# Turned products of the last two channel groups laid out by partition in DRAM, and read back by four transfers each

## The chip, the cores and the metric

The kernel runs on one core of one Trainium2 chip. The metric is device time in microseconds (us), the median of several executions; before the change it is 266.08 us (three runs, 264.74 to 267.07). The core has a matrix engine (PE, with its weight loads shown apart as PEld), a vector engine (DVE), a scalar engine (ACT), GpSimd (POOL) and a sync engine (SP), which here issues nearly all transfers; sixteen DMA engines carry them.

## The reference

Two branches work on the same input of 2048 positions by 512 channels, and a gate per position mixes them. Branch a convolves each channel with a kernel built from 128 complex exponentials; branch b is linear attention with 32 heads.

```python
x = A_u
g = _sigmoid((x * gate_w).sum(-1, keepdims=True))
P = jnp.exp(logdA[:, :, None] * l[None, None, :])
K = jnp.einsum("dn,dnl,dn->dl", Cc, P, dB).real
...
y = irfft2(rfft2(u, padded) * rfft2(K, padded))[..., :L] + u * Dskip
...
b = _B_ref(x, B_wqkv, B_w_phi, B_wo)
return g * a + (1 - g) * b
```

## The kernel before

The convolution is done by a Fourier transform in two stages of matrix products. The 512 channels are worked in quarters Q of 128; units of 32 channels (0 to 15) make the convolution kernels (`kgen`), and `transform` carries a group of channels through the rest. The first three quarters go as groups of nd = 128 channels. The last quarter is cut into three groups by `g.LAST`: units 12 and 13 (nd = 64), unit 14 (nd = 32), both "far", and unit 15 (nd = 32), "near".

In `transform` a group goes through these steps, named as the profile names their tiles:

- `psB` on PE (L192), copied to `XK`, multiplied on DVE with the spectrum of the input, `XUX`, to give `t` (L1231, for nd = 32 in two halves, L1234). `XUX` is loaded from DRAM by `load`, two transfers of 256 KB for each of four parts of a quarter (L1183, for the last quarter L1185, where each of 128 partitions takes one run of 2 KB).
- `psz` on PE (L1263) is the first stage of the inverse transform, evicted by ACT to `Zr`. For a far group the product has to be turned: what lies in one partition as many rows r has to lie with r over the partitions. This goes through DRAM: `fw` writes `Zr` to the tensor `Zd` (L1277 or L1279), `fr` reads `Zd` back into `ZT` (L1290 or L1292). A group of nd channels has 1024/nd rows r in one write, so nd = 64 makes two writes and nd = 32 one. The near group takes another way (L1304) and has no round trip.
- `psy` on PE (L1342, L1348) is the second stage, from `ZT`; DVE multiplies by the gate into `xT` (L1373), and `st` writes the result to `out` (L1387). The attention part of the output is written by L992.

In 128 partitions p stands for the pair (x, t), x of 4 and t of 32. Before the change the two layouts of `Zd` are: for nd = 128 and 64 ("byrow") [r, x, t, d], written in runs of nd numbers and read by four transfers of 32 partitions, each partition one long run; for nd = 32 [t, x, r, d], written with x as the outermost of two partition dimensions and read by two transfers of 64 partitions.

The order of all work is written out by hand: `Plan` holds a list of nodes and the string `ORDER`, and every engine issues its instructions in that order. SP therefore takes transfers strictly one after another; a transfer whose wait isn't met holds those behind it. Eight completion semaphores are handed round among the transfers, so a transfer can also wait for the one eight places ahead of it. `XUX` has three buffers, `Zr` two and `ZT` one (shared with another tile, "ax").

Of the kernel before, what the change touches and what calls it, by code (L numbers as in the profile page):

```python
# [13 lines left out]
BF16 = mybir.dt.bfloat16  # L14
# [1042 lines left out]
def plan_conv(P, nc, g, psum, r):  # L1057
# [8 lines left out]
    def evict2(name, get, deps, ps):  # L1066
        out = []
        for k in range(2):
            out.append(P.add(("ACT", "DVE"), name, lambda k=k: P.copy(*get(k)), [ps] + deps[k] + out, drop=(["psum"] if k else [])))
        return out  # L1070
# [119 lines left out]
    def transform(XA, ready, Q, off, nd, far, Ls, last, co=0, free=True, split=False):  # L1190

        F = Bag()
        ng, ns, nj, nt = nd // 2, 1024 // nd, min(16, 1024 // nd) if far else 8, min(32, 2048 // nd)
# [4 lines left out]
        ov = g.out2d[:, 128 * (Q - pair) + lo:128 * Q + off + nd].rearrange("(q j c) d -> c q j d", q=32, j=16, c=4)  # L1198
        bS = xT[:, :, Q, :]
        if far:  # L1200
            byrow = nd > 32
            F.Zd = g.dram.tile([32, 4, 32, nd], BF16, name=f"Zd{Q}_{off}")
        tn, zn, rn, wn = [], [], [], []
        for r0 in range(0, 32, ns):
            box = Bag()
# [44 lines left out]
            x = evict2("XK", xk, [[], []], b) if split else [evict("XK", xk, [b])]  # L1250
# [24 lines left out]
            def fw(r0=r0, box=box):  # L1275
                if byrow:
                    nc.sync.dma_start(out=F.Zd[r0:r0 + ns].rearrange("r x t d -> (x t) r d"), in_=box.Z[:])  # L1277
                else:
                    nc.sync.dma_start(out=F.Zd[:, :, r0:r0 + ns, :].rearrange("t x r d -> x t (r d)"), in_=box.Z[:].rearrange("p r d -> p (r d)"))  # L1279
                box.Z = None  # L1280
            z = P.add("PE", "psz", fi, [tn[-1]] + ([z] if r0 else []), take=[psq, "Zr"], drop=(["r8"] if (r0 + ns) % nt == 0 else []), rw=("TI", ""))
            zn.append(evict("Zr", fe, [z] + zn[-1:]))
            wn.append(P.dma("zw", 0.45, 2.0, fw, [zn[-1]], drop=["Zr"], move=0.9))

        def fr(th):
            if th == 0:
                F.Z = g.fpool.tile([128, 4096], BF16, name="ZT", tag="ax", bufs=g.P.k["ax"])[:, 0:32 * nd].rearrange("p (t d) -> p t d", d=nd)
            if byrow:
                for x in (2 * th, 2 * th + 1):
                    nc.sync.dma_start(out=F.Z[32 * x:32 * x + 32], in_=F.Zd[:, x])  # L1290
            else:
                nc.sync.dma_start(out=F.Z[64 * th:64 * th + 64], in_=F.Zd[:, 2 * th:2 * th + 2].rearrange("t x r d -> (x r) t d"))  # L1292
        for th in range(2 if far else 0):
            rn.append(P.dma("zr", 0.6, 2.0, lambda th=th: fr(th), wn + [n.issue for n in rn[-1:]], take=(["ax"] if th == 0 else []), move=max(1.2, 2.8 * nd / 128 + 0.1), cnt=2 if byrow else 1))
        box = Bag()

        def iz(k2, box=box):
# [23 lines left out]
        for j0 in range(0, 16, nj):  # L1321
            box = Bag()
# [66 lines left out]
            if Q < 3:  # L1389
                ya = [P.add("PE", "pya", pya, [sq] + [n for b in range(j0 // 4, min(3, j0 // 4 + 2)) for n in g.ot[b]] + ([y] if j0 else []), take=[psq], rw=("diagD", ""))]  # L1390
            y = P.add("PE", ("psy%d" if far else "psyn%d") % nd, py, ya + (rn[:1 + (j0 + nj - 1) // 8] if far else zn) + [sq] + (late if Q == 3 else []) + ([y] if j0 else []),
                      take=[] if ya else [psq],
# [11 lines left out]
    for h in range(6):  # L1404
        for u in (2 * h, 2 * h + 1):
            if u in g.PHASES and u:
                phase(range(u, g.PHASES[u]))
        if h % 2 == 0:
            XA = Bag()
            XA.nd, XA.off, XA.drop, done = 128, 0, True, []  # L1410
        done = done + kgen((2 * h, 2 * h + 1), XA, h % 2 == 0)
        if h % 2:
            transform(XA, done, h // 2, 0, 128, True, [load(h // 2, p) for p in range(4)], False)
# [7 lines left out]
    for k, (units, far) in enumerate(g.LAST):  # L1421
        XA = Bag()
        XA.nd, XA.off, XA.first = 32 * len(units), 32 * (units[0] - 12), first
        XA.drop = units[-1] == 15
        done = kgen(units, XA, True, units in g.SPLIT)
        first = XA.first
        end = units[-1] == 15
        off = 32 * (units[0] - 12)
        transform(XA, done, 3, off, XA.nd, far, L[off // 64 * 2:off // 64 * 2 + 2], end, off % 64, units[-1] % 2 == 1, units in g.SPLIT)
# [204 lines left out]
```

## Time and profile before

| | before |
|---|---|
| median of the runs | 266.08 us (264.74 to 267.07) |
| profiled execution: device time | 267.7 us |
| profiled execution: span, first to last instruction | 265.9 us |
| mean granted PE clock | 0.923 |
| busy share of the span: DVE, ACT, PE | 87%, 83%, 74% |
| DMA: moved, mean rate | 36.19 MB, 136 GB/s |
| DMA packets, of them under 512 bytes | 67087, 46308 |

The span is what the views of the profile divide up; 1.8 us of the device time lie outside it. All times in a view count from the span's start. DVE and ACT are busy nine tenths of the time up to about 240 us; the last 25 us have low shares on every engine, and there the chain of waits goes over transfers and PE.

### The profile page before, as it was taken

The numbers are of one execution on the slowest core, as the hardware profiler recorded it, in microseconds if no ns is written. First come the engines' busy times: TensorE is split into PE (matmuls) and PEld (weight loads), VectorE is DVE, ScalarE is ACT, GpSimd is POOL, SyncE is SP. The second block draws the span as 40 slices with busy tenths as digits, with TensorE's granted clock in tenths as the row PEclk, the third lists the DMA queues.
The fourth block names the chain that finished last, engine by engine and source line by source line (L and its number), as shares of the span: only waits on it lengthen the run. The fifth ranks groups of instructions, "written<-read, shape, count | busy, mean of one in ns | idle before, by whom it ended". The sixth has DMA issues, their size and how long they took to land.

```text
span 265.9 us, 10075 instructions
## 1 busy us (share of the span) xinstructions
PE 195.7 (74%) x4492; PEld 134.0 (50%) x4512; DVE 231.8 (87%) x314; ACT 221.2 (83%) x305; POOL 11.7 (4%) x22
## 2 busy tenths in 40 slices
PE   0386899999947568887487666799886787993840
PEld 0275566755735333445355354575764566762630
DVE  6899799898799998999999999999999999934440
ACT  7877998888899999999999999999999988553000
POOL 4750000000000000000000000000000000000000
PEclk9997999999985798999959999999999999999575
DMA  6799000361721677406150575639775989586675
GB/s 193 132 202 208 1 4 2 115 160 39 226 61 58 177 223 206 137 6 164 48 148 7 156 194 147 154 88 231 189 210 129 217 207 223 94 218 146 140 92 90
DMA packets 67087, 36.19 MB, mean 136 GB/s; under 512 B 46308, under 2 KB 62820, under 8 KB 66660
## 3 DMA queue, kind: packets, MB, share of 16 engines
q1 hardware_dynamic: 65988, 35.42, 55.0%
q8 instruction: 35, 0.57, 1.0%
q10 hardware_dynamic: 1056, 0.13, 0.3%
q14 instruction: 8, 0.07, 0.1%
HBM read 22.17 MB, written 13.37 MB: 134 GB/s over the span
## 4 chain that ended last, share of the span: by engine, by line
DVE 30%; ACT 27%; PE 27%; issue 6%; DMA 6%; SPq 1%; DVEq 0%; ACTq 0%
ACT cs L68 6%; DMA XUX<-XUd 6%; PE pk L705 5%; PE vp L753 4%; DVE A L1098 3%; DVE t L1231 3%; ACT E L68 3%; ACT XA L145 3%; ACT Eq L68 3%; PE psB L612 2%; PE kvp L770 2%; ACT L65 2%; PE psA L587 2%; ACT XK L145 2%; DVE XAu L147 2%
## 5 line engine op out<-in xcount | busy, mean ns | idle before, releaser
L1098 DVE TENSOR_TENSOR A<-Ctab,Dtab 128x2048 bf16<-128x2048 bf16 x32 | 38.6, 1218 | 0.4 <-PE kps L179 0.4
L68 ACT ACTIVATE cs<-args 128x1024 bf16<-128x1024 f32 x32 | 31.0, 1072 | 0.0
L179 PE MATMUL kps<-R,A 128*32 128x64 bf16 x1536 | 17.3, 201 | 5.9 <-DVE A L1098 1.8
L179 PEld LDWEIGHTS <-A 128*32 128x32 bf16 x1536 | 15.6, 116 | 10.1 <-issue 4.1
L1116 DVE TENSOR_TENSOR R<-E,cs 128x2048 bf16<-128x2048 bf16 x16 | 19.5, 1218 | 0.6 <-ACT E L68 0.5
L1120 DVE TENSOR_TENSOR R<-E,cs 128x2048 bf16<-128x2048 bf16 x16 | 19.5, 1216 | 0.0
L145 ACT CAST Zr<-psz 128x1024 bf16<-128x1024 f32 x15 | 15.6, 1040 | 4.3 <-issue 3.4
L1263 PE MATMUL psz<-t,TI 128*128 128x512 bf16 x53 | 14.8, 379 | 5.7 <-DVE t L1234 2.6
L68 ACT ACTIVATE Ek<-pk 128x512 bf16<-128x512 f32 x32 | 16.7, 603 | 2.6 <-PE pk L705 2.5
L145 ACT CAST XA<-psA 128x1024 bf16<-128x1024 f32 x15 | 15.1, 1043 | 3.1 <-PE psA L186 3.1
L1231 DVE TENSOR_TENSOR t<-XUX,XK 128x2048 bf16<-128x2048 bf16 x14 | 16.9, 1216 | 0.4 <-ACT XK L145 0.4
L753 PE MATMUL vp<-WW,xT 128*128 128x512 bf16 x58 | 16.3, 406 | 1.0 <-issue 0.8
L68 ACT ACTIVATE E<-args 128x1024 bf16<-128x1024 f32 x16 | 16.8, 1059 | 0.2 <-PE args L1042 0.2
L68 ACT ACTIVATE Eq<-pq 128x512 bf16<-128x512 f32 (+1 forms) x28 | 16.6, 698 | 0.1
L839 PE MATMUL pq<-xT,Wqp 128*128 128x512 bf16 x64 | 16.3, 392 | 0.6 <-ACT Eq L68 0.6
L145 ACT CAST XK<-psB 128x1024 bf16<-128x1024 f32 x15 | 15.2, 1024 | 1.6 <-PE psB L192 1.5
L612 PE MATMUL psB<-XAu,TB 64*128 64x128 bf16 x256 | 11.3, 248 | 5.8 <-ACT xst L145 4.0
L705 PE MATMUL pk<-WW,xT 128*128 128x512 bf16 x58 | 14.7, 380 | 0.4 <-issue 0.2
L186 PE MATMUL psA<-W,KD 128*64 128x128 bf16 x256 | 10.9, 232 | 5.6 <-ACT cs L68 3.5
L612 PEld LDWEIGHTS <-TB 64*128 64x128 bf16 x256 | 9.5, 110 | 9.0 <-issue 8.9
L192 PE MATMUL psB<-XA,TB 128*128 128x128 bf16 (+2 forms) x192 | 10.2, 202 | 5.1 <-DVE XA L147 1.7
L186 PEld LDWEIGHTS <-KD 128*64 128x64 bf16 x256 | 8.9, 116 | 8.7 <-issue 6.6
(210 smaller groups left out, 503.4 us busy)
## 6 DMA issues: line engine op xcount, KB each, us to landing
XUX<-XUd SPq DMA_DIRECT2D x32, 256.0 KB, 4.4
XUd<-xst SPq DMA_DIRECT2D x8, 512.0 KB, 3.0
ax<-apd SPq DMA_DIRECT2D x16, 256.0 KB, 4.5
Zd<-Zr SPq DMA_DIRECT2D x15, 256.0 KB, 3.2
ZT<-Zd SPq DMA_DIRECT2D x12, 256.0 KB, 4.9
UD<-in_A_u_dram SPq DMA_DIRECT2D x16, 128.0 KB, 4.2
XUd<-xst SPq DMA_DIRECT2D x8, 256.0 KB, 3.8
wqk<-in_B_wqkv_dram SPq DMA_DIRECT2D x1, 1024.0 KB, 6.5
```

What stands on the lines that cost most here:

```text
L68: return self.nc.scalar.activation(**kw)
L145: self.nc.scalar.copy(out=o, in_=i)
L179: nc.tensor.matmul(kps[32 * dj:32 * dj + 32, g4, e, :], lhsT=A[:, d // 4, 32 * ka:32 * ka + 32, d % 4], rhs=R[:, kr, d, :], start=(i == 0) ...
L186: nc.tensor.matmul(ps[64 * ri:64 * ri + 64], lhsT=lhsT, rhs=fc.W1[:, ri].rearrange("p r d -> p (r d)"), start=True, stop=True, tile_positi ...
L612: nc.tensor.matmul(box.ps[:, c2, sl, :], lhsT=fc.TB[rows, b0:b0 + 2].rearrange("p a b -> p (a b)"), rhs=X.t[rows, k, r0 + sl].rearrange("p ...
L705: nc.tensor.matmul(box.ps[:], lhsT=xT[:, st, kt, :], rhs=g.WW[:, kt, :], start=(kt == 0), stop=(kt == 3))
L753: nc.tensor.matmul(box.ps[:], lhsT=xT[:, st, kt, :], rhs=g.WW[:, 4 + kt, :], start=(kt == 0), stop=(kt == 3))
L839: nc.tensor.matmul(box.ps[:, m - m0, :] if late else box.ps[:], lhsT=g.Wqp[:, kt, 128 * m:128 * m + 128], rhs=xT[:, 4 * b:4 * b + 4, kt, : ...
L1098: nc.vector.tensor_tensor(out=c.A[:, :, 64 * k:64 * k + 64, :].rearrange("p q (x b) l -> p x b q l", b=8), in0=cf.unsqueeze(2).to_broadcas ...
L1116: nc.vector.tensor_tensor(out=c.R[:, :, :, 32:64], in0=t.E[:, 1].unsqueeze(1).to_broadcast([128, 2, 32, 32]), in1=t.cs[:], op=ALU.mult)
L1120: nc.vector.tensor_tensor(out=c.R[:, :, :, 0:32], in0=t.E[:, 0].unsqueeze(1).to_broadcast([128, 2, 32, 32]), in1=t.cs[:, ::-1, :, ::-1], o ...
L1231: nc.vector.tensor_tensor(out=box.t, in0=Ls[r0 // ns].X[:], in1=box.XK[:].unsqueeze(1).to_broadcast([128, 2, 1024]), op=ALU.mult)
```

## The change

The diff touches only the far groups of fewer than 128 channels, so the three transfers of `Zr` of the last quarter's first two groups (two writes for nd = 64, one for nd = 32) and what reads them back. `Zd` is now [x, t, r, d] for both: the partition is outermost and one dimension, a partition's rows and channels are one run. It is read by four transfers of 32 partitions, one for each x, in which every partition gathers 32 runs of nd numbers. For nd = 128 nothing changes.

```diff
-            byrow = nd > 32
-            F.Zd = g.dram.tile([32, 4, 32, nd], BF16, name=f"Zd{Q}_{off}")
+            byrow = nd > 64
+            F.Zd = g.dram.tile([32, 4, 32, nd] if byrow else [4, 32, 32, nd], BF16, name=f"Zd{Q}_{off}")
...
                 if byrow:
                     nc.sync.dma_start(out=F.Zd[r0:r0 + ns].rearrange("r x t d -> (x t) r d"), in_=box.Z[:])
                 else:
-                    nc.sync.dma_start(out=F.Zd[:, :, r0:r0 + ns, :].rearrange("t x r d -> x t (r d)"), in_=box.Z[:].rearrange("p r d -> p (r d)"))
+                    nc.sync.dma_start(out=F.Zd[:, :, r0:r0 + ns, :].rearrange("x t r d -> (x t) r d"), in_=box.Z[:])
...
-            if byrow:
-                for x in (2 * th, 2 * th + 1):
-                    nc.sync.dma_start(out=F.Z[32 * x:32 * x + 32], in_=F.Zd[:, x])
-            else:
-                nc.sync.dma_start(out=F.Z[64 * th:64 * th + 64], in_=F.Zd[:, 2 * th:2 * th + 2].rearrange("t x r d -> (x r) t d"))
+            for x in (2 * th, 2 * th + 1):
+                nc.sync.dma_start(out=F.Z[32 * x:32 * x + 32], in_=F.Zd[:, x] if byrow else F.Zd[x].rearrange("t r d -> r t d"))
```

No compute instruction moves. On SP's queue, towards the end, the rows before are these; `Zd_0_122` is the DRAM tensor of the group of 64 channels, `Zd_64_123` that of the far group of 32, and the shape is that of the transfer's pattern (partitions or runs first, the run last):

```order
L1277 DMA Zd_0_122<-Zr 128x16x64 x2
L1185 DMA XUX<-XUd 128x1024 x4
L1290 DMA ZT<-Zd_0_122 32x2048 x4
L1387 DMA out_dram<-xT 32x12x256 x2
L1387 DMA out_dram<-xT 32x12x128 x2
L1279 DMA Zd_64_123<-Zr 4x32x1024
L1387 DMA out_dram<-xT 32x12x256 x2
L992 DMA out_dram<-xT 32x4x384 x2
L1292 DMA ZT<-Zd_64_123 64x32x32 x2
L1387 DMA out_dram<-xT 32x12x128 x2
```

At the same place of SP's queue after the change (lines below the diff have numbers smaller by 3):

```order
L1279 DMA Zd_0_122<-Zr 128x1024 x2
L1185 DMA XUX<-XUd 128x1024 x4
L1289 DMA ZT<-Zd_0_122 32x32x64 x4
L1384 DMA out_dram<-xT 32x12x256 x2
L1384 DMA out_dram<-xT 32x12x128 x2
L1279 DMA Zd_64_123<-Zr 128x1024
L1384 DMA out_dram<-xT 32x12x256 x2
L992 DMA out_dram<-xT 32x4x384 x2
L1289 DMA ZT<-Zd_64_123 32x32x32 x4
L1384 DMA out_dram<-xT 32x12x128 x2
```

Every write of `Zd` now has runs of 1024 numbers (2 KB) and 128 of them outermost; the four reads of the group of 64 have runs of 64 numbers (128 bytes) instead of 2048 (4 KB); the reads of the group of 32 keep their runs of 32 numbers (64 bytes) but are four instead of two, so two issues are added on SP.

More of the change, by code (lines that the diff above doesn't have):

```diff
@@ L1287, in fr @@
                 F.Z = g.fpool.tile([128, 4096], BF16, name="ZT", tag="ax", bufs=g.P.k["ax"])[:, 0:32 * nd].rearrange("p (t d) -> p t d", d=nd)
-            if byrow:
-                for x in (2 * th, 2 * th + 1):
-                    nc.sync.dma_start(out=F.Z[32 * x:32 * x + 32], in_=F.Zd[:, x])
-            else:
-                nc.sync.dma_start(out=F.Z[64 * th:64 * th + 64], in_=F.Zd[:, 2 * th:2 * th + 2].rearrange("t x r d -> (x r) t d"))
+            for x in (2 * th, 2 * th + 1):
+                nc.sync.dma_start(out=F.Z[32 * x:32 * x + 32], in_=F.Zd[:, x] if byrow else F.Zd[x].rearrange("t r d -> r t d"))
         for th in range(2 if far else 0):
-            rn.append(P.dma("zr", 0.6, 2.0, lambda th=th: fr(th), wn + [n.issue for n in rn[-1:]], take=(["ax"] if th == 0 else []), move=max(1.2, 2.8 * nd / 128 + 0.1), cnt=2 if byrow else 1))
+            rn.append(P.dma("zr", 0.6, 2.0, lambda th=th: fr(th), wn + [n.issue for n in rn[-1:]], take=(["ax"] if th == 0 else []), move=max(1.2, 2.8 * nd / 128 + 0.1), cnt=2))
         box = Bag()
```

## The prediction

> **What bounds the kernel now.** I read the chain of waits first, then SP's part of the timeline, then DMA counts for stretches of it. Over the whole span the chain is spread over engines:
>
> ```profile
> span 265.9 us, 10075 instructions
> DVE 30%; ACT 27%; PE 27%; issue 6%; DMA 6%; SPq 1%; DVEq 0%; ACTq 0%
> ```
>
> The change acts from 230 us on, so only the end counts. The chain there (start, length, what):
>
> ```profile
> 232.49 1.98 SPq L1185
> ...
> 235.47 6.86 DMA XUX<-XUd
> ...
> 242.42 0.69 DVE t L1234
> 243.11 1.14 DVE xT L1373
> 244.25 1.20 DVE XA L147 x2
> ...
> 245.49 1.02 PE psB L192 x32
> ...
> 249.34 3.63 PE psz L1304 x123
> ...
> 257.70 0.82 PE psy L1348 x50
> ...
> 258.54 0.69 DVE xT L1373
> ```
>
> From 232.5 to 242.3 the kernel waits for one thing: the issue and landing of four XUX loads, which `t` of the group of 32 needs. The rest is a dependent chain up to the last `xT`, ending at 259.23. SP's own rows show why XUX is late, and a second queue behind it:
>
> ```profile
> 230.04 1.79 SPq L1277 DMA_DIRECT2D Zd<-Zr  x2
> 231.92 3.97 SPq L1185 DMA_DIRECT2D XUX<-XUd  x4
> 236.48 3.38 SPq L1290 DMA_DIRECT2D ZT<-Zd  x4
> 240.28 4.82 SPq L1387 DMA_DIRECT2D out_dram<-xT  x4
> 245.20 0.65 SPq L1279 DMA_DIRECT2D Zd<-Zr  x1
> 245.90 1.02 SPq L1387 DMA_DIRECT2D out_dram<-xT  x2
> 247.02 4.00 SPq L992 DMA_DIRECT2D out_dram<-xT  x2
> 251.12 2.21 SPq L1292 DMA_DIRECT2D ZT<-Zd  x2
> 253.38 7.58 SPq L1387 DMA_DIRECT2D out_dram<-xT  x6
> 261.00 1.13 SPq L992 DMA_DIRECT2D out_dram<-xT  x2
> 262.23 1.25 SPq L1387 DMA_DIRECT2D out_dram<-xT  x2
> ```
>
> SP issues its last transfer until 263.48, 4.25 us after the last `xT`, and the span ends 2.43 us after that. So the end is set by SP and the DMA queues, not by compute: SP is nearly without a gap from 245.20 on, and its start there hangs on XUX. Its queue takes in turn: Zd of the 32 (245.20), two L992 at 2.0 us each, the ZT reads, and eight outputs plus two L992.
>
> **The writes of the 64.** Each of the two writes has 128 x 16 = 2,048 runs of 128 bytes, 4,096 together. Between 230.9 and 235.0 the DMA view counts on SP's queue (packets, MB, share of the DMA engines)
>
> ```profile
> q1 hardware_dynamic: 4074, 0.52, 83.8%
> ```
>
> and the windows view gives, for that stretch and the one behind it (PE, PEld, DVE, ACT, POOL, then clock, DMA share, GB/s),
>
> ```profile
> 230.90:235.00 4.10, 4.10 (x158) 3.64 (x156) 2.86 (x4) 2.08 (x3) 0.00 (x0) 1.00 0.86 130
> 235.00:239.40 4.40, 4.35 (x32) 2.14 (x24) 1.12 (x2) 2.15 (x5) 0.00 (x0) 1.00 0.90 270
> ```
>
> That is 4.1 us for half a megabyte, with the engines full and XUX queued behind: its data cannot begin before 235. XUX itself moves in packets of 2 KB, at 270 GB/s. The changed writes have the same packet size, 256 packets and 0.52 MB, so 0.52 / 0.27 = 1.9 us (estimate) instead of 4.1: 2.2 us less. They can't begin before their issue: the second follows ACT's eviction of its half,
>
> ```profile
> 230.38 1.03 ACT L145 CAST Zr<-psz 128x1024 bf16<-128x1024 f32 x1
> ```
>
> so it is issued after 231.41; from issue to data took 0.86 (230.04 to 230.9), and half of 1.9 behind that puts its data at about 232.3 to 233.3, where XUX begins. XUX also loses its stalled issue:
>
> ```profile
> L1185 SPq DMA_DIRECT2D XUX<-XUd x8: 376/432/2545, 212.4 to 235.5; - x8
> DMA to landing us min/median/max: 2.9/4.4/6.9
> ```
>
> (issue in ns, least, median, most; then issue to landing). The 2,545 is the first issue behind the 4,096 packets; the median is 432. Four at 0.43 from 231.92 begin the last at 233.25 instead of 235.47: 2.2 us, the same size as the transport gain, as they are one queue seen from its two ends and not two gains. Landing: 6.86 at worst and 4.4 at the median, so the last lands between 237.7 and 240.1 instead of 242.3, 2.2 to 4.7 us earlier. I take 3.0, nearer to the low end: the stretch from 239.5 to 242.3 still carried a few late XUX packets at a DMA rate that had fallen,
>
> ```profile
> 239.50:242.30 2.80, 1.11 (x19) 0.62 (x19) 0.00 (x0) 0.85 (x2) 0.00 (x0) 1.00 0.81 190
> ```
>
> and whatever made those late is not in the diff. PE's own work caps the gain: XA needs `psA` of unit 15, which PE does after the attention output,
>
> ```profile
> 239.43 0.64 PE L186 MATMUL psA<-W,KD 128*64 128x128 bf16 x16
> ```
>
> so XA can't begin before 240.1, against 244.25: at most 4.1.
>
> **The reads of the 64.** They were 32 x 4 = 128 runs of 4 KB and become 4,096 runs of 128 bytes. The trace has no such read. Nearest rows: the 4,074 written packets of 128 bytes in 4.1 us above, and the reads of 64-byte runs of the 32, also 4,096, between 252.5 and 256.3:
>
> ```profile
> q1 hardware_dynamic: 4086, 0.26, 68.9%
> ```
>
> That is 3.8 us at the most, since PE's fetches and outputs lie in it. So 3.6 to 4.1 us; I take 3.8, against 0.52 MB at 270 GB/s = 1.9 before. They are issued behind XUX, so they delay no XUX packet; after XUX (done at about 237 on most engines) they occupy the queue until about 241. Their consumer stands at
>
> ```profile
> 247.28 0.89 PE L1348 MATMUL psy<-ZT,TJ 64*32 64x64 bf16 x64
> ```
>
> and would come at 244.3; that is cover enough. The outputs of L1387 at 240.28 queue behind them, but there SP stood waiting,
>
> ```profile
> SPq L1387 <- DVE xT L1373: 2.6, 1, 2.6
> ```
>
> (total, times, longest), until `xT` was done at 244.25, which becomes 241.3. So I cost this edit at nothing; without that cover it costs the difference of 3.8 and 1.9, some 2 us, on Zd of the 32. Below nothing it cannot be: no piece gets larger.
>
> **The write of the 32.** SP comes to it after four outputs, the last two waiting for `xT`, so with `t` 3.0 us earlier it is issued at 242.2 instead of 245.2 (Zr is evicted by ACT just before). It has 128 runs of 2 KB both before and after, but was laid out as 4 x 32. Little moved behind its issue, and the two L992 behind it took 4.00 us where the same pair took 1.13 at 261.00. The DMA share shortly after was
>
> ```profile
> 246.40:246.80 0.40, 0.40 (x6) 0.05 (x2) 0.26 (x1) 0.00 (x0) 0.00 (x0) 0.50 0.29 50
> ```
>
> about four to five engines of sixteen at work with 256 KB queued. The Trainium skill, "DMA: Bandwidth & Descriptors", in the section on why a DMA increments its semaphore by 16, has a transfer use the largest count up to 16 that divides the outermost dimension of both sides: 4 before, 16 after. The share agrees. By the rows alone, if the write kept its time, only the 3.0 of `t` would reach the ZT reads. With all engines at work the write behaves as those of L1277:
>
> ```profile
> L1277 SPq DMA_DIRECT2D Zd<-Zr x14: 359/371/591, 153.2 to 231.4; - x14
> DMA to landing us min/median/max: 2.7/3.2/6.4
> ```
>
> It was followed by its readers 5.92 us after its issue (251.12 - 245.20). Now: SP needs 0.65 + 1.02 + 1.13 and 0.2 of gaps after the issue, so it stands at the ZT reads at 245.2; the write lands at 242.2 + 3.2 = 245.4 by the median and 248.6 by the worst. Two queued outputs of 192 KB lie ahead and beside, so I take 246.5. The ZT reads start 4.6 us earlier; bounds 5.9 (245.2, SP alone) and, with the XUX gain of 2.2 and the landing of 6.4, 251.12 - 249.4 = 1.7.
>
> **The reads of the 32.** The runs stay, the transfers become four. Two issues are added on SP, in front of ten more issues. The two now (issue in ns, then landing):
>
> ```profile
> L1292 SPq DMA_DIRECT2D ZT<-Zd x2: 647/1084/1522, 251.1 to 251.8; - x2
> DMA to landing us min/median/max: 4.1/4.7/5.2
> ```
>
> The second's 1,522 I read as waiting for room in the queue. A plain issue of 0.43 to 0.65 each gives +0.9 to +1.3, I take 1.1; nothing, if SP is held there by the same 4,096 packets anyway. The Trainium skill, same page, "Rules for kernel authors", speaks against splitting a transfer over disjoint partition halves, as both use the same engines; by it the four reads bring nothing over two, and the sum stays as it is, since I count no gain for them.
>
> **The compute behind.** The last `xT` needs ZT of the 32: reads at 246.5, the last issued some 1.5 later and landing 4.1 to 5.2 after that, `psy` about 252.5 instead of 257.7. The chain over `psz` L1304 moves by 3.0 with `t`. Both stay ahead of SP's last two issues, which had 3 us of slack. PE's clock was about half there,
>
> ```profile
> 245.50:252.50 7.00, 5.83 (x222) 4.86 (x223) 2.67 (x4) 0.00 (x0) 0.00 (x0) 0.51 0.73 144
> ```
>
> behind the wait for XUX; with a shorter wait it may stay up and L1304 be shorter. As SP sets the end, I count nothing for it.
>
> **The sum.** ZT reads of the 32 begin 4.6 us earlier, two more issues cost 1.1: 3.5 us off the end. Span 265.9 - 3.5 = 262.4, device time of a profiled execution 267.7 - 3.5 = 264.2. The median of the runs lies 1.6 below the profiled execution, so 266.08 - 3.5 = 262.6. Bounds: 5.9 with hidden issues gives 260.2; 1.7 less 1.3 gives 0.4, so 265.7.
>
> **The rivals.** (1) The gain stays at the front: XUX lands with its worst latency of 6.86, the reads of the 64 with their 3.8 us hold the write of the 32 back, and SP's end moves by 0.4 to 2: 264.1 to 265.7, say 265.0. For it speaks that the last XUX took 6.86, though by 239.4 the engines had moved 1.19 MB (4.4 us at 270 GB/s) for its four loads of 1 MB; against it the 4.1 us of writes that surely leave its queue. Chance 0.24. (2) More: the added issues vanish in the stall at the ZT reads and the write lands as fast as SP gets there, 260.2 to 261.2. Chance 0.10; the stalls of 2 us in SP's rows speak for it, the outputs queued around the write against it. (3) Slower: the cost of issuing reads made of many pieces. If each of the four reads of the 32 holds SP as long as the second did, 1.52 us (1,522 ns), they take 6.1 instead of 2.2, 3.9 more on the queue that sets the end; the four reads of the 64 take 6.1 instead of 3.4 and eat SP's idle time. It makes the kernel slower by over 1% once the front gains under 1.2 us; with 1.0 gained it is 269.0. Against it: the pieces per transfer are halved, and the 0.65 of the first read. Chance 0.08. (4) The writes are split as before, or the rows are of no matter to DMA time, and nothing moves: 266.1; the pattern 128x1024 speaks against it. Chance 0.02.
>
> **The numbers.** A change under 1%, 2.7 us, can't be told from none here. The forecast, 262.6 with 261.2 to 264.2, has 0.56, of which 0.06 lies above 263.4. Faster by over 1%: 0.50 + 0.10 = 0.60. Within 1%: 0.06 + 0.24 + 0.02 = 0.32. Slower: 0.08. The range 260.2 to 265.7 takes in the bounds of the sum and rival (1); outside are rivals (3) and (4) and about 0.08 of the tails.
>
> **What would show it.** Right: the four XUX issues take about 1.7 us from 231.9, `t` L1234 runs at about 239.4, the two L992 about 1.1 to 1.6, the first ZT read of the 32 at 246 to 247. Wrong: `t` still at 242; the reads of the 64 landing after 244; issues of 1.5 us each for all ZT reads; or SP idle at the end with PE or DVE last.

## The result and the profile after

The changed kernel takes 263.42 us (median of 20 runs, 262.36 to 265.59); the kernel before, on the same chip, 267.16 (20 runs, 264.74 to 268.80). The ratio is 0.9865 with a 95% interval of 0.9841 to 0.9888: 3.6 us faster by the ratio (3.7 between the medians), where 3.5 was predicted. (Runs that a slower state of the chip disturbed are left out of every comparison here.) The profiled execution took 265.59 us; its page:

```profile
span 263.8 us, 10077 instructions
ACT 31%; PE 30%; DVE 22%; issue 7%; DMA 6%; POOL 1%; SPq 1%; ACTq 0%; DVEq 0%; POOLq 0%
```

SP's queue from the first write of the group of 64 on (start, length; the lines of the last part of the program have numbers smaller by 3):

```profile
231.93 1.74 SPq L1279 DMA_DIRECT2D Zd<-Zr  x2
233.77 1.83 SPq L1185 DMA_DIRECT2D XUX<-XUd  x4
235.92 5.20 SPq L1289 DMA_DIRECT2D ZT<-Zd  x4
241.54 3.31 SPq L1384 DMA_DIRECT2D out_dram<-xT  x4
244.95 0.59 SPq L1279 DMA_DIRECT2D Zd<-Zr  x1
245.58 1.19 SPq L1384 DMA_DIRECT2D out_dram<-xT  x2
246.88 2.01 SPq L992 DMA_DIRECT2D out_dram<-xT  x2
249.00 2.98 SPq L1289 DMA_DIRECT2D ZT<-Zd  x4
252.02 6.80 SPq L1384 DMA_DIRECT2D out_dram<-xT  x6
258.87 1.11 SPq L992 DMA_DIRECT2D out_dram<-xT  x2
260.07 1.25 SPq L1384 DMA_DIRECT2D out_dram<-xT  x2
```

The first write lies at 231.93 here and at 230.04 before. Nothing that the change touches comes earlier in the program, and in the other profiles below it lies between 229.1 and 230.8; executions differ that much ahead of it. So the readings here count from the first write of the 64, the zero of every "after the first write" below. From it to the end of the span: before 265.9 - 230.04 = 35.9, now 263.8 - 231.93 = 31.9. Two more profiles of the changed kernel gave 31.8 and 32.1, so 0.3 is about what this stretch can tell. The kernel before was profiled once. In eleven of the thirteen profiles of the kernels here, the gain in this stretch is larger than the timed gain, by 1.05 us in the mean of all thirteen; so the stretch may be longer in that one execution than it commonly is, and gains read against it may be up to about 1 us too large (an estimate).

The chain of waits of the changed kernel, in the same stretch:

```profile
235.16 6.18 DMA XUX<-XUd
...
241.44 0.69 DVE t L1234
242.13 1.14 DVE xT L1370
243.26 1.21 DVE XA L147 x2
...
248.30 3.11 PE psz L1301 x124
...
256.19 0.69 DVE xT L1370
```

Counted from the first write, the steps stand so:

| step | before | after | gain |
|---|---|---|---|
| last XUX issued | 5.4 | 3.2 | 2.2 |
| second `t` of the 32 begins | 12.4 | 9.5 | 2.9 |
| write of the 32 issued | 15.2 | 13.0 | 2.1 |
| its first reader issued | 21.1 | 17.1 | 4.0 |
| SP's last issue done | 33.4 | 29.4 | 4.1 |
| end of the span | 35.9 | 31.9 | 4.0 |

The gain arises in two places: 2.9 us at `t`, and 1.9 us between the write of the 32 and its readers (5.9 to 4.05). Of the first, 0.7 is lost again before that write.

### The profile page after: what moved, and what is told of

The parts are those of the page before. It is cut to its first block, busy times and chain, and to the rows that moved or that the text cites. A ratio compares the mean times of both kernels' runs of the same rounds, so it can differ in the third digit from the quotient of the medians.

```text
span 263.8 us, 10077 instructions
## 1 busy us (share of the span) xinstructions
PE 199.0 (75%) x4492; PEld 135.1 (51%) x4512; DVE 231.0 (88%) x314; ACT 221.2 (84%) x305; POOL 11.4 (4%) x22
## 4 chain that ended last, share of the span: by engine, by line
ACT 31%; PE 30%; DVE 22%; issue 7%; DMA 6%; POOL 1%; SPq 1%; ACTq 0%; DVEq 0%; POOLq 0%
ACT cs L68 6%; PE pk L705 5%; DMA XUX<-XUd 5%; PE vp L753 4%; ACT E L68 3%; PE psz L1263 3%; ACT Eq L68 3%; ACT XK L145 3%; ACT XA L145 2%; ACT Zr L145 2%; ACT xst L145 2%; PE kvp L770 2%; ACT L65 2%; PE psA L587 2%; PE psA L186 2%
## 5 line engine op out<-in xcount | busy, mean ns | idle before, releaser
L179 PE MATMUL kps<-R,A 128*32 128x64 bf16 x1536 | 18.3, 205 | 6.9 <-issue 2.0
L179 PEld LDWEIGHTS <-A 128*32 128x32 bf16 x1536 | 16.2, 118 | 11.6 <-issue 5.9
L145 ACT CAST XA<-psA 128x1024 bf16<-128x1024 f32 x15 | 15.2, 1040 | 3.3 <-PE psA L186 3.3
L1263 PE MATMUL psz<-t,TI 128*128 128x512 bf16 x53 | 16.0, 412 | 2.2 <-DVE xT L1370 0.6
L145 ACT CAST XK<-psB 128x1024 bf16<-128x1024 f32 x15 | 15.3, 1024 | 1.6 <-PE psB L192 1.5
L612 PE MATMUL psB<-XAu,TB 64*128 64x128 bf16 x256 | 11.3, 248 | 5.8 <-ACT xst L145 3.9
L192 PE MATMUL psB<-XA,TB 128*128 128x128 bf16 (+2 forms) x192 | 10.2, 201 | 4.9 <-DVE XA L147 1.6
```

The costliest lines, as they stand in the source:

```text
L145: self.nc.scalar.copy(out=o, in_=i)
L179: nc.tensor.matmul(kps[32 * dj:32 * dj + 32, g4, e, :], lhsT=A[:, d // 4, 32 * ka:32 * ka + 32, d % 4], rhs=R[:, kr, d, :], start=(i == 0) ...
L612: nc.tensor.matmul(box.ps[:, c2, sl, :], lhsT=fc.TB[rows, b0:b0 + 2].rearrange("p a b -> p (a b)"), rhs=X.t[rows, k, r0 + sl].rearrange("p ...
L1263: nc.tensor.matmul(box.ps[:, hb, :], lhsT=fc.TIp[:, k].rearrange("p h a t -> p (h a t)"), rhs=box.t[:, k, 512 * hb:512 * hb + 512], start= ...
```

## The experiments

My theory: two gains in series on SP's queue, XUX let through by the shorter writes of the 64, and the write of the 32 spread over all engines. Rivals: all of it is the one, or all of it is the other. Each kernel was timed in five rounds beside the kernel before.

### Only the group of 64

```diff
-            F.Zd = g.dram.tile([32, 4, 32, nd] if byrow else [4, 32, 32, nd], BF16, name=f"Zd{Q}_{off}")
+            F.Zd = g.dram.tile([4, 32, 32, nd] if nd == 64 else [32, 4, 32, nd], BF16, name=f"Zd{Q}_{off}")
...
-                else:
+                elif nd == 64:
                     nc.sync.dma_start(out=F.Zd[:, :, r0:r0 + ns, :].rearrange("x t r d -> (x t) r d"), in_=box.Z[:])
+                else:
+                    nc.sync.dma_start(out=F.Zd[:, :, r0:r0 + ns, :].rearrange("t x r d -> x t (r d)"), in_=box.Z[:].rearrange("p r d -> p (r d)"))
...
+            if nd == 32:
+                nc.sync.dma_start(out=F.Z[64 * th:64 * th + 64], in_=F.Zd[:, 2 * th:2 * th + 2].rearrange("t x r d -> (x r) t d"))
+                return
```

> Only the group of 64 takes the new layout (two writes in 2 KB runs, four reads in 128-byte runs); the far group of 32 stays as before, written 4 x 32 and read by two transfers. My theory is that the change is two gains in series on SP's queue: XUX landing about 2.9 us earlier after the first write of the 64 (9.5 instead of 12.4 us from that write to the second t of the 32), of which 2.1 reach the issue of the write of the 32, and 1.9 more at the write of the 32 itself. Then this kernel keeps the first: about 2.1 us, ratio to the kernel before 0.992, with the write of the 32 still taking 5.9 us to its readers and the two L992 about 4 us. Rival A, all the gain is XUX: ratio 0.986, as the whole change. Rival B, all the gain is the write of the 32, since compute isn't what ends the kernel: ratio 1.000.

Ratio 0.9952 (0.9927 to 0.9978). SP's rows:

```profile
230.52 1.74 SPq L1279 DMA_DIRECT2D Zd<-Zr  x2
...
243.09 0.65 SPq L1281 DMA_DIRECT2D Zd<-Zr  x1
...
245.36 4.06 SPq L992 DMA_DIRECT2D out_dram<-xT  x2
249.87 2.05 SPq L1291 DMA_DIRECT2D ZT<-Zd  x2
```

The write of the 32 comes 12.6 after the first write, the readers 6.8 behind it, the two L992 take 4.06, and the span (264.2) ends 33.7 after the first write: 2.2 gained in the profile, 1.3 in the timed runs. Both rivals fall: it is neither all nor nothing. My own 0.992 lies just outside the interval too: the write comes 2.6 earlier, but its readers follow by 6.8 and not 5.9, so 1.7 of that reaches them.

### Only the far group of 32

```diff
-            byrow = nd > 64
+            byrow = nd > 32
```

> Only the far group of 32 takes the new layout (one outermost dimension of 128 in the write, four reads); the group of 64 stays as before. Two gains in series: this one keeps the second, about 1.9 us, ratio 0.993; the second t of the 32 still comes about 12.4 us after the first write of the 64, the two L992 take about 2 us instead of 4, and the readers follow the write of the 32 by about 4 us instead of 5.9. Rival A, all is XUX: 1.000. Rival B, all is the write of the 32: 0.986.

Ratio 0.9954 (0.9922 to 0.9987). SP's rows and, below, what SP waited for from 248 us on (total, times, longest):

```profile
229.85 1.79 SPq L1277 DMA_DIRECT2D Zd<-Zr  x2
...
244.94 0.43 SPq L1279 DMA_DIRECT2D Zd<-Zr  x1
...
246.50 1.91 SPq L992 DMA_DIRECT2D out_dram<-xT  x2
248.51 3.07 SPq L1289 DMA_DIRECT2D ZT<-Zd  x4
```

```profile
SPq L1384 <- DVE xT L1373: 2.6, 1, 2.6
```

The L992 take 1.91 instead of 4.00 and the readers follow the write after 3.6, so the step itself gains 2.3, more than the 1.9 I expected. But the span (264.8) ends 35.0 after the first write, only 0.9 earlier: SP runs ahead and then waits 2.6 us for `xT`. That `xT` is done 25.4 after the first write, as in the kernel before: without XUX earlier, compute is what is late next. So in the profiles the parts don't simply add: 2.2 and 0.9 alone, 4.0 together. The timed runs don't show it firmly: 0.9952 times 0.9954 is 0.9906, the whole gave 0.9865, 0.9896 and 0.9852, and each interval reaches 0.002 to 0.004 to either side.

### The write of the 32 in four transfers

```diff
-                    nc.sync.dma_start(out=F.Zd[:, :, r0:r0 + ns, :].rearrange("t x r d -> x t (r d)"), in_=box.Z[:].rearrange("p r d -> p (r d)"))
+                    for x in range(4):
+                        nc.sync.dma_start(out=F.Zd[:, x, r0:r0 + ns, :].rearrange("t r d -> t (r d)"), in_=box.Z[32 * x:32 * x + 32].rearrange("p r d -> p (r d)"))
```

> The kernel before, with its old layout and its two reads for the far group of 32, but the write of that group cut into four transfers of 32 partitions, one for each x, so that no transfer has a dimension of 4 outermost. Three issues are added on SP ahead of the outputs. If the slow write was slow because its outermost dimension was 4, it now spreads over all engines and gains as the one of 128 does, 1.9 us less 0 to 1.5 for the issues: ratio 0.993 to 0.999, with the two L992 near 2 us or less. If what helped was the new order of the bytes in DRAM or the four reads, the L992 stay near 4 us and the ratio is 1.000 to 1.006.

Ratio 0.9972 (0.9942 to 1.0003). SP's rows:

```profile
230.13 1.79 SPq L1277 DMA_DIRECT2D Zd<-Zr  x2
...
245.34 1.75 SPq L1280 DMA_DIRECT2D Zd<-Zr  x4
247.13 0.97 SPq L1388 DMA_DIRECT2D out_dram<-xT  x2
248.19 1.63 SPq L992 DMA_DIRECT2D out_dram<-xT  x2
249.93 2.47 SPq L1293 DMA_DIRECT2D ZT<-Zd  x2
```

Layout and reads are the old ones, and yet the L992 take 1.63, and the readers come 4.6 after the first of the four writes, although three issues were added. So the slow write came from its outermost dimension of 4, not from where the bytes lie nor from the number of reads. The trace's completion events say the same. The old write of the 32 has five events, in the kernel before and in the two others here that keep it; before, one comes soon after its issue (246.23 us) and four come with the data (250.51 to 250.96). In the changed kernel sixteen come with the data (247.41 to 248.50), and each of the four writes here has sixteen. By the Trainium skill, "DMA: Bandwidth & Descriptors", in the section on why a DMA increments its semaphore by 16, a transfer on four engines is counted twelve at its issue and once more by each engine as its data lands. The trace agrees: one event and four. The span (265.1) ends 35.0 after the first write, 0.9 earlier than before; the timed gain, 0.3%, has an interval that reaches 1.

### XUX ahead of the writes of the 64, no layout changed

```diff
+L1185 DMA XUX<-XUd 128x1024 x4
 L1277 DMA Zd_0_122<-Zr 128x16x64 x2
-L1185 DMA XUX<-XUd 128x1024 x4
```

> The kernel before with no layout changed; on SP the four last XUX loads are issued ahead of the two writes of the group of 64 instead of behind them (their buffers are free from about 228 us). If XUX was late because it lay in the queue behind 4,096 packets of 128 bytes, the second t of the 32 now comes within about 7 us of the first write of the 64 (DVE's own work is then what is ahead of it) instead of 12.4, XA waits for PE's psA instead, the write of the 32 is issued about 2.9 us earlier, and the ratio is about 0.989. If XUX is late for another reason (a DMA engine shared with instruction fetches, memory), t gains under 1 us and the ratio is 0.997 to 1.000.

Ratio 0.9944 (0.9913 to 0.9974), where I had expected 0.989. SP's rows, and below them DVE's two `t` in this kernel:

```profile
223.57 4.11 SPq L1185 DMA_DIRECT2D XUX<-XUd  x4
230.39 2.74 SPq L1277 DMA_DIRECT2D Zd<-Zr  x2
...
243.37 0.67 SPq L1279 DMA_DIRECT2D Zd<-Zr  x1
```

```profile
235.81 1.28 DVE L1234 TENSOR_TENSOR t<-XUX,XK 128x1024 bf16<-128x1024 bf16 x2
```

The second `t` is done 6.7 after the first write (10.2 in the change) and its wait for XUX is gone. XUX is issued 8.7 us earlier here, so this run alone can't tell the 4,096 packets from another cause of delay. The profiles with XUX behind the writes can: the last XUX is complete 12.2 to 12.3 after the first write in the three that have the old writes of the 64 ahead of it (the kernel before, the far group alone, the four transfers), and 8.7 to 9.5 after it in the seven with the new writes. The write of the 32 comes at 13.0, as in the changed kernel, and the span (263.7) ends at 33.3. So a `t` another 3.5 us earlier gains nothing at that write: its data (`Zr`) is evicted 12.1 after the first write in this profile and in those of the change alike. It needs `psz` (L1263), which stands behind `psA` in PE's order, and `psA` behind the attention output; I had named `psA` as the cap for `XA` alone.

### The reads of the 64 in long runs

```diff
-F.Zd[x].rearrange("t r d -> r t d")
+(F.Zd[x] if nd == 64 else F.Zd[x].rearrange("t r d -> r t d"))
```

> The change itself once more, as the measure for the three kernels beside it. All theories: ratio 0.9865 within 0.3%, and from the first write of the 64 to the end of the span 31.9 us (before 35.9).

> The change, but the four reads of the group of 64 take each partition as one run of 4 KB, as the kernel before read them: they return rows that aren't turned, so the turn of that group is left out of the computation. It shows what the 4,096 runs of 128 bytes cost where they now lie. My theory after the result: they cost about 0.9 us, since SP is held 3.2 us at the third read, reaches the outputs late and issues the write of the 32 at 13.0 us after the first write of the 64 where its data was ready at 12.1: ratio about 0.983. My prediction's theory: they cost nothing, 0.9865. A rival in which the small reads also hold up the later outputs and instruction fetches: under 0.980.

The change gave 0.9896 (0.9854 to 0.9937), the kernel with long runs 0.9892 (0.9846 to 0.9938), on the same chip: no difference. In its profile the write of the 32 is issued on time, and the reads of the 32 start 15.9 after the first write, 1.6 earlier than in the change beside it (17.5):

```profile
229.80 1.74 SPq L1279 DMA_DIRECT2D Zd<-Zr  x2
...
234.71 1.71 SPq L1289 DMA_DIRECT2D ZT<-Zd  x4
...
241.98 0.43 SPq L1279 DMA_DIRECT2D Zd<-Zr  x1
...
245.67 3.20 SPq L1289 DMA_DIRECT2D ZT<-Zd  x4
```

What SP waited for from 248 us on:

```profile
SPq L1384 <- DVE xT L1373: 1.7, 1, 1.7
SPq L1384 <- DMA out_dram<-xT: 1.4, 1, 1.4
```

The lead goes into waits for `xT` and for the landing of an earlier output, whose semaphore is used again. The short reads do cost SP's queue what I said after the result (0.7 to 1.0 at the write of the 32), but the end doesn't feel it, and my 0.983 was wrong.

### Eight reads of the 32

```diff
-                nc.sync.dma_start(out=F.Z[32 * x:32 * x + 32], in_=F.Zd[x].rearrange("t r d -> r t d"))
+                for h in range(2):
+                    nc.sync.dma_start(out=F.Z[32 * x + 16 * h:32 * x + 16 * h + 16], in_=F.Zd[x, :, 16 * h:16 * h + 16].rearrange("t r d -> r t d"))
```

> The change, with the far group of 32 read back by eight transfers of 16 partitions instead of four of 32: same runs, four more issues on SP. My prediction priced a further issue at about 0.55 us: that gives 2.2 us more, ratio 0.995. The profile of the change says that issues at this place vanish, as SP is held afterwards until the reads' data has moved: ratio 0.9865 to 0.9885, and from the first read to SP's last issue 12.3 us as in the change and before.

> The kernel with eight reads of the far group of 32 once more: its timed ratio (0.9952) and its profiled end (32.1 us after the first write of the 64, 0.3 more than the change) don't agree. If four more issues cost about 0.55 each on the queue that ends last, ratio 0.993 to 0.997 again and an end near 34; if they vanish in the stall behind them, 0.985 to 0.990 and an end near 32.

Ratios 0.9952 (0.9920 to 0.9984) and 0.9910 (0.9875 to 0.9945). The rows of the first:

```profile
248.05 5.05 SPq L1291 DMA_DIRECT2D ZT<-Zd  x8
253.15 4.63 SPq L1388 DMA_DIRECT2D out_dram<-xT  x6
...
259.05 1.25 SPq L1388 DMA_DIRECT2D out_dram<-xT  x2
```

Eight issues take 5.05 where the four of the change took 2.98, but the outputs behind take 4.63 where they took 6.80. From the first read to SP's last issue it is 260.30 - 248.05 = 12.25, in the second profile 11.9; in the kernel before 12.35; in the three profiles of the change 12.3, 11.8 and 12.7. By the profiles four more issues cost nothing that shows, as SP's next issues are then held less. The timed runs say otherwise. On the chip of the first, the medians are 265.26 us with eight reads (12 runs) and 263.11 with the change (6 runs), and 11 of the 12 lie above the slowest of the 6: 2.15 us, about the 0.55 an issue of my prediction. The second ratio, on another chip, lies 0.1 to 0.6% above those of the change. Of the 1.6 us between the profiled executions on the first chip, 1.2 lies ahead of the first write, where the edit changes nothing. So what an issue costs here stays open, between nothing and about 0.5 us.

### XUX ahead, with the layouts

```diff
+L1185 DMA XUX<-XUd 128x1024 x4
 L1279 DMA Zd_0_122<-Zr 128x1024 x2
-L1185 DMA XUX<-XUd 128x1024 x4
```

> The change, and on SP the four last XUX loads ahead of the two writes of the group of 64. t comes at about 6 us after the first write of the 64 instead of 9.5, and the reads of the 64 are no longer queued behind XUX. What is ready last for the write of the 32 is then the eviction of its Zr at 12.1, which has not moved in any run with t early: the write of the 32 can gain 0.9 us at most, from SP being free earlier: ratio about 0.983. If the write of the 32 isn't what the end hangs on, the gain is that of compute, 1.2 us at XA, or nothing: 0.982 to 0.9865.

The change with XUX moved ahead as above gave 0.9882 (0.9841 to 0.9923) beside the change's 0.9896; my 0.983 lies outside that interval. Its write of the 32 is issued 12.1 after the first write, as soon as `Zr` is there, and its span ends 30.3 after the first write, 1.5 earlier than the change. The two below, and the change a third time, ran on one chip.

> The change itself on the chip of the two kernels beside it: ratio 0.9865 to 0.9896, from the first write of the 64 to the end of the span 31.8 to 31.9 us.

The next has the edit of the far group alone (`byrow = nd > 32`), with XUX moved ahead of the old writes of the 64:

```diff
+L1185 DMA XUX<-XUd 128x1024 x4
 L1277 DMA Zd_0_122<-Zr 128x16x64 x2
-L1185 DMA XUX<-XUd 128x1024 x4
```

> The kernel before with the new layout for the far group of 32 alone, and with the four last XUX loads ahead of the writes of the group of 64, which keep their 128-byte runs and their 4 KB reads. If the layout of the 64 helps only by letting XUX through, this does as well as the whole change, without its reads in short runs: the write of the 32 issued at 12.1 to 13.0 us after the first write of the 64, ZT read at 15.9 to 17, end at 31 to 32, ratio 0.983 to 0.990. If the new layout of the 64 has a worth of its own, the ratio stays near that of the far group alone with XUX late, 0.995.

The last is the change with XUX ahead and two more moves on SP:

```diff
 L1384 DMA out_dram<-xT 32x12x256 x2
+L1279 DMA Zd_64_123<-Zr 128x1024
 L1384 DMA out_dram<-xT 32x12x128 x2
-L1279 DMA Zd_64_123<-Zr 128x1024
...
+L992 DMA out_dram<-xT 32x4x384 x2
 L1384 DMA out_dram<-xT 512x1x64 x4
-L992 DMA out_dram<-xT 32x4x384 x2
```

> The change with three groups of transfers moved on SP: the four last XUX loads ahead of the writes of the 64; the write of the 32 ahead of the two outputs that wait for xT; the last two transfers of the attention output ahead of the outputs of the 64, where SP stood waiting 1.7 us for xT with XUX moved alone. The write of the 32 can't be issued before its Zr at 12.1 (it was at 12.12 with XUX moved alone), so the second move gives at most 0.3; the third fills up to 1.1 of the 1.7. End at 29.2 to 30.3 us after the first write of the 64 (31.8 with the change, 30.3 with XUX moved alone), ratio 0.980 to 0.987. If compute now sets the end, the third move gives nothing: 30.3, 0.988.

| kernel | ratio (95% interval) | end after the first write, us |
|---|---|---|
| the change, third time | 0.9852 (0.9812 to 0.9893) | 32.1 |
| XUX ahead, new layout for the 32 alone | 0.9835 (0.9791 to 0.9879) | 30.3 |
| the change, three groups of transfers moved | 0.9846 (0.9806 to 0.9887) | 30.9 |

The rows of the second:

```profile
229.10 2.98 SPq L1277 DMA_DIRECT2D Zd<-Zr  x2
...
242.25 0.62 SPq L1279 DMA_DIRECT2D Zd<-Zr  x1
...
246.69 3.05 SPq L1289 DMA_DIRECT2D ZT<-Zd  x4
249.78 4.31 SPq L1384 DMA_DIRECT2D out_dram<-xT  x6
```

With XUX out of the way the group of 64 can keep its short writes and its long reads, and the kernel is as fast as with the whole change: 261.99 us against 262.73, which the intervals don't part. The layout of the 64 helped by letting XUX through and has no other worth that shows here. The third kernel's two further moves brought nothing that shows (262.38 us); its last `xT` ends no earlier (24.2 after the first write in both). No kernel here is shown to beat the change. The three with XUX ahead and the new layout of the 32 aren't shown to be worse, and their profiled ends lie 0.9 to 1.8 us earlier.

## Why the prediction was right, and where its terms were off

The forecast of 262.6 from 266.08 is a ratio of 0.987; measured were 0.9865, 0.9896 and 0.9852. That a change under 1% can't be told from none was too careful for 20 runs of each: their interval reaches 0.0024 to either side. Step by step, from the first write:

- **XUX.** Four issues in 1.83 us (predicted about 1.7), the stall of 2.5 gone; `t` 2.9 earlier (predicted 3.0). The last landing took 6.18, so it did stay near the worst of the old rows, as I had assumed when I took the low end. Right, and the last landings with the old and the new writes ahead (12.2 to 12.3 against 8.7 to 9.5) show the cause. That it was 3.0 was a choice between 2.2 and 4.7, with the late XUX packets unexplained; the hit is in part luck.
- **The reads of the 64.** This is the step that failed: "So I cost this edit at nothing". Counted from the first write, their packets were to have moved by 11.0 (the prediction's 241). All but a few had moved by 11.4, and they took some 5.2 us, not 3.8, by the packets on SP's queue between 238 and 243.3. SP was held 3.2 us at the third read (issue in ns, least, median, most):

```profile
q1 hardware_dynamic: 4282, 0.72, 99.4%
```

```profile
L1289 SPq DMA_DIRECT2D ZT<-Zd x20: 318/528/3227, 174.6 to 251.4; - x20
```

  That hold was over before `xT` was done (11.3 after the first write), so it was covered, as I had said. What wasn't covered is the tail: the last of these packets moved at 11.7, and the first output queued behind them landed from 12.5 on, while the two outputs that wait for `xT`, just ahead of the write of the 32, were issued from 11.4. Those two took 1.56 us in the change (first row) and 0.83 with the reads in long runs (second row):

```profile
243.29 1.56 SPq L1384 DMA_DIRECT2D out_dram<-xT  x2
```

```profile
241.05 0.83 SPq L1384 DMA_DIRECT2D out_dram<-xT  x2
```

  So the write of the 32 gained 2.1 (2.0 and 2.3 in the other two profiles of the change) instead of 3.0. That the backlog of the queue made these issues longer is read from these rows. I had looked for the cover of the reads' consumer and not for what an issue costs behind a full queue, though the 2,545 ns in a row that I quoted was just that. The time didn't hang on it: with long runs the kernel was no faster.
- **The write of the 32.** Readers 4.05 behind it (4.3 and 4.0 in the others), predicted 4.3. The L992 took 2.01, not 1.1 to 1.6, which I had from a later pair of that line. The number of engines, taken from the Trainium skill's rule, is shown by the completion events and by the write in four transfers. The share of busy engines rose from 0.29, 1.2 us after the write's issue, to 0.77, 1.45 us after it:

```profile
246.40:246.80 0.40, 0.12 (x14) 0.01 (x1) 0.40 (x1) 0.00 (x0) 0.00 (x0) 1.00 0.77 126
```

- **Two more issues.** I priced them at 1.1; the profiles show 0 within about 0.5: the stretch from the first read to SP's last issue is 12.3 as before (11.8 and 12.7 in the other two profiles of the change). That was the first half of rival (2). The timed runs of the eight reads leave a price like mine open. The Trainium skill's rule on two transfers to disjoint partition halves (same page, "Rules for kernel authors") gives a split no gain, and none shows here.
- **The sum.** 4.6 - 1.1 = 3.5 was 4.0 - 0 = 4.0 in the profile: two errors of about 0.6 and 1.1 that partly cancel. The total was right in part by that luck. The timed gain, 3.6, doesn't say how it is made up.
- **Who sets the end.** SP still issues last, 4.4 us after the last `xT`. But the claim that compute doesn't matter holds only as long as both move: in the far group alone SP waited 2.6 us for `xT`. Gains in front and behind need each other, which the sum didn't say.
- **PE's clock** stayed low over the last `psz`: granted 0.62 over L1301 (3.11 us), 0.57 over L1304 before (3.63 us). I had counted nothing for it.

Rival (1) had two of its parts, the late last XUX and the short reads that hold back the write of the 32, but at 0.7 to 1.0 us they were too small for its 265.0; (3) is refuted for the reads of the 32, which took 0.56 to 1.02 each. Its other half, 6.1 for the four reads of the 64, came close (5.20, and 6.05 and 5.16 in the other two profiles of the change); most of that lay ahead of `xT`. (4) is refuted by everything above.

## What to carry to other kernels

A transfer of many short runs is paid for by what is issued behind it, in the DMA queue and on the issuing engine; look for whose load that is, and whether reordering the two issues does as much as a new layout. Look at the outermost dimension of each transfer: here the readers followed a write with 4 outermost after 5.9 us, one with 128 after 4.05, and four writes with 32 after 4.6. When two queues of waits run side by side to the end, shortening one gains only until the other is late, so parts tried alone can understate the whole.

## What the runs showed of the hardware that was not expected

Reads of 128-byte runs from DRAM were slow at first: between 239 and 241 us the engines were full and moved 101 GB/s, while at 241 to 243.2 the same transfers moved 129. Why the first half is slower was not tried.

```profile
239.00:241.00 2.00, 2.00 (x13) 0.94 (x11) 0.50 (x1) 1.32 (x3) 0.00 (x0) 1.00 1.16 101
241.00:243.20 2.20, 1.93 (x23) 0.98 (x22) 1.76 (x3) 1.04 (x3) 0.00 (x0) 1.00 0.88 129
```

And the last XUX load hung on one of its sixteen completions: in the kernel before, fifteen of its sixteen completions came between 238.83 and 240.54 and the last at 242.33; in the changed kernel fifteen between 238.28 and 240.59, the last at 241.34. In all ten profiles with XUX behind the writes the last came 0.4 to 1.9 us after the fifteenth. A PE instruction fetch of 16 KB took 1.81 us at 237.7 in the kernel before; that it is this fetch which holds up that completion is a guess.
